# Reading the moving columns of the feed-forward matmuls alternately from the two halves of the operand

## The chip, the cores and the metric

The kernel runs on one core of one Trainium2 chip. The metric is the device time of one execution in microseconds (us), the median of several runs. Beside it stands one execution taken by the hardware profiler, which gives the time of every instruction on each engine: TensorE (PE, with its weight loads as PEld), VectorE (DVE), ScalarE (ACT), GpSimd (POOL) and SyncE (SP), which issues the DMAs.

## The reference

Two stages follow each other. The first is an attention through 32 inducing points over x (4 batches, 12416 rows, 128 channels). The second is a gated feed-forward on its 49664 rows, with 1536 hidden units:

```python
scale = 1.0 / np.sqrt(C)
def mab(q, kv):
    s = scale * (q @ kv.transpose(0, 2, 1))
    s = s - s.max(-1, keepdims=True)
    a = np.exp(s)
    a /= a.sum(-1, keepdims=True) + 1e-09
    return a @ kv
h = mab(I, x)            # 32 inducing rows look at all rows of x
x = mab(x, h).reshape(B * S, D)
g = x @ w_gate
silu = g * (1.0 / (1.0 + np.exp(-g)))
val = x @ w_val
return (silu * val) @ w_out
```

Every row (token) goes through the feed-forward by itself: the order of the tokens does not matter to the arithmetic, so long as the output is put back in order.

## The kernel before

**Layout.** In the feed-forward a token is a column. The attention output is not formed: the 32 weights of a token over the inducing points are put, split in a high and a low part for the 4 row groups, into a tile `stack` of 128 partitions, and the 32 inducing rows are multiplied into the gate and value weights beforehand (tile `tw`, called `st.w`). A matmul of `stack` (the moving operand, streamed column by column) against a 128x128 block of `tw` (the stationary operand, loaded ahead by PEld) gives 128 hidden units of 512 or 480 tokens.

**Tiling.** Each batch has 25 column blocks: 13 of 512 tokens (the first one has 4 x 128) and then 12 of 480. Each block is multiplied in `NT` = 12 steps of 128 hidden units. One such step is a slot:

- `front` (L680) issues two matmuls, the gate (L691) and the value (L692); both read `stack`.
- `gate` has ACT take the SiLU of the gate out of PSUM (L697); `value` has DVE multiply it by the value (L705), which gives `h`.
- `split` rounds `h` to the short format fp32r in `h_hi` (L713, mostly ACT) and subtracts to get the rest, `h_lo` (L715, mostly POOL, one slot in four DVE).
- `back` (L719) issues three matmuls that accumulate in one PSUM tile `o`: `wo_lo` by `h_hi` (L729), `wo_hi` by `h_hi` (L730) and `wo_hi` by `h_lo` (L731). After 12 steps `evac` has DVE copy `o` to `ob` (L738), and SP writes it out.

All five of these matmuls have fp32r operands. The very first block of batch 0 (`u.whole`) is different: its output product is one plain fp32 matmul for each step (L727), which stands in the trace as two MATMUL records.

The moving operands lie without gaps: column k of `stack`, `h_hi` or `h_lo` is the word after column k-1 in each partition. Their tiles are 64 columns wider than needed (`WB`), and start 0 to 48 columns into them, by the table `AT`.

**Order.** The order of the instructions on each engine is written out in the program: slot by slot `front`, `gate`, `value` and the `split` of the slot before, then pieces of the next batch's attention from a list with due slots, then `back` for a slot some 5 to 10 slots older. The first block has its order in the text `SECOND`. Nothing in this order depends on how an operand is addressed. The rest of PE's work is attention: transposes of x (L262), scores (L270), sums over rows (L318, L371) and the projection of the weights (L398, L420).

**Output.** Each block is written as 128 rows of n tokens, and the host's Python turns the blocks into (tokens, 128).

Of the kernel before, what the change touches and what calls it, by code (L numbers as in the profile page):

```python
# [17 lines left out]
B, N, C, M, DFF = 4, 12416, 128, 32, 1536  # L18
P = 128
NG = 4  # L20
NTB = N // NG // 32


def starts(sizes):
# [10 lines left out]
WF = 32 * max(FC)  # L35
WB = WF + 64
AT = (16, 48, 48), (0, 32, 16)
NT = DFF // P
# [14 lines left out]
WP = 512  # L53
# [52 lines left out]
def induced_set_attention_then_swiglu(ctx: ExitStack, tc: tile.TileContext, xt, xn, ind, wgv, wo, out):  # L106
    nc = tc.nc
# [44 lines left out]
    def wcol(k, t):  # L152
        at = WP * (t // 2) + 2 * P * k + P * (t % 2)
        return slice(at, at + P)

    wgv_sb = const.tile([P, 2 * DFF], F32, name="wgv_sb")
    wo_hi = const.tile([P, DFF], F32R, name="wo_hi")
    wo_lo = const.tile([P, DFF], F32R, name="wo_lo")
# [39 lines left out]
    def at(u):  # L198

        return AT[u > NG * FC.count(max(FC))]  # L200
# [10 lines left out]
    def attention(b, one, xn0=None, xt0=None):  # L211
# [5 lines left out]
        def psum(second=0):  # L217
            if xn0 is not None or second:
                return ps_gv.tile([P, 512], F32, name="gv")
            return ps_o.tile([P, 512], F32, name="o")  # L220
# [53 lines left out]
        def s1(q, second=0):  # L274
            if q == 0:
                st.s = one.tile([P, NTB * 32], F32, name="s_all")
                st.mx = att.tile([P, NCH], F32, name="mx")
# [84 lines left out]
        def hacc2(q):  # L362
            g = q >= GA
            n0, n1 = (0, CH0[GA])[g], (CH0[GA], NTB)[g]
            if q in (0, GA):
# [65 lines left out]
        def sl2(b0, b1):  # L431
            return st.s2[:, b0:b1, :]

        def s2_m(b0, b1, second=0):
            if not hasattr(st, "s2"):
                st.s2 = one.tile([P, NTB, M], F32, name="s_all")
            st.sp[b0] = psum(second)
# [16 lines left out]

        def exp2(b0=0, b1=NTB):
            nc.scalar.activation(out=sl2(b0, b1), in_=sl2(b0, b1), func=AF.Exp)
# [166 lines left out]
    start = tc.manual_schedule()  # L623
    start.__enter__()
    s_all = oneb.tile([P, NTB * 32], F32, name="s_all")
    with tc.tile_pool(name="xt0", bufs=NCH - NXT) as xt0, tc.tile_pool(name="xn0", bufs=NCH - NXN) as xn0:
        cur = attention(0, one, xn0, xt0)
        f = cur.f
# [3 lines left out]
        pieces = {}  # L632
# [11 lines left out]
        def run(token):  # L644
            name, *args = token.split(":")
            args = [int(x) if x.isdigit() else x for x in args]
            if name == "ld":
                load_piece(*args)
            elif args and args[0] in pieces:
                getattr(pieces[args[0]], name)(*args[1:])  # L650
            else:
                short[name](*args)
# [27 lines left out]
    def front(st, b, c, t):  # L680
        u = Tile()
        q, j = COLS[c]
        u.b, u.q, u.j, u.t = b, q, j, t
        u.at = at(c)
        n = u.n = WF if q == 0 else 32 * FC[q]

        u.whole = b == 0 and c == 0
        rhs = st.stack[c][:, :n]
        u.g = ps_gv.tile([P, 512], F32, name="gv")
        u.v = ps_gv.tile([P, 512], F32, name="gv")  # L690
        nc.tensor.matmul(out=u.g[:, :n], lhsT=st.w[:, wcol(0, t)], rhs=rhs, start=True, stop=True)  # L691
        nc.tensor.matmul(out=u.v[:, :n], lhsT=st.w[:, wcol(1, t)], rhs=rhs, start=True, stop=True)  # L692
        return u
# [25 lines left out]
    def back(u):  # L719
        n, t = u.n, u.t  # L720
        if t == 0:
            acc["o"] = ps_o.tile([P, 512], F32, name="o")
        o = acc["o"]
        ws = slice(P * t, P * t + P)
        if u.whole:
            k = t % (WP // P)
            nc.tensor.matmul(out=o[:, :n], lhsT=pieces[f"o{t // (WP // P)}"].w[:, P * k:P * k + P], rhs=u.h[:, :n], start=(t == 0), stop=(t == NT - 1))  # L727
        else:
            nc.tensor.matmul(out=o[:, :n], lhsT=wo_lo[:, ws], rhs=u.hi[:, :n], start=(t == 0), stop=False)  # L729
            nc.tensor.matmul(out=o[:, :n], lhsT=wo_hi[:, ws], rhs=u.hi[:, :n], start=False, stop=False)  # L730
            nc.tensor.matmul(out=o[:, :n], lhsT=wo_hi[:, ws], rhs=u.lo[:, :n], start=False, stop=(t == NT - 1))  # L731
        if t == NT - 1:
            evac(u, o)

    def evac(u, o):
        n = u.n
        ob = obp.tile([P, WF], F32, name="ob")
        nc.vector.tensor_copy(out=ob[:, :n], in_=o[:, :n])  # L738
        at = NG * 32 * FC0[u.q] + u.j * n
        nc.sync.dma_start(out=out[u.b, P * at:P * (at + n)].rearrange("(d t) -> d t", d=P), in_=ob[:, :n])  # L740
# [6 lines left out]
    def first(t):  # L747
        made.append(front(cur, 0, 0, t))
        pend.append(made[t])

    short |= dict(f=first, g=lambda t: gate(made[t]), m=lambda t: value(made[t]), k=lambda t: back(pend.pop(0)))
    for token in SECOND.split():
        run(token)
    cur.steps = [(slot, lambda token=token: run(token)) for slot, tokens in FIRST.items() for token in tokens.split()]
    ahead = len(pend)
    for b in range(B):
        nxt = attention(b + 1, (one, oneb)[(b + 1) % 2]) if b + 1 < B else None
        if nxt is not None:
            nxt.steps = plan(nxt, PA if b == 0 else PB)
            if b == 0:  # L760
                cur.steps.append((nxt.e1, lambda: run(f"e2:52:{NTB}")))
                for q in range(2, NF):
# [6 lines left out]
        for slot in range(NT if b == 0 else 0, SLOTS):  # L769
            c, t = slot // NT, slot % NT  # L770
            u = front(cur, b, c, t)
            gate(u)
            value(u)
            u.cast_dve = t in CAST
            u.last = b == B - 1 and slot == SLOTS - 1
            if wait:
                split(wait[0])
                pend.append(wait.pop(0))
            wait.append(u)
            if slot in bursts:  # L780
                u.cast_dve = True
                split(u)
                pend.append(wait.pop(0))
            for a in (cur, nxt):
                while a is not None and a.steps and a.steps[0][0] <= slot:

                    if pend and pend[0].t in getattr(a.steps[0][1], "acc", ()):
                        break
                    a.steps.pop(0)[1]()
            ahead = min(ahead + 1 / RAMP, HI) if nxt is not None and slot < last_burst else max(ahead - 1 / RAMP, SKEW)  # L790
            if slot in bursts:
                ahead = SKEW - (b == 0)
            while len(pend) + len(wait) > ahead:
                back(pend.pop(0))
# [5 lines left out]
    for u in pend + wait:  # L800
        back(u)
# [37 lines left out]
```

## Time and profile before

| | |
|---|---|
| median of 3 runs | 1459.46 us (1459.44 to 1459.61) |
| profiled execution | 1459.38 us |
| its span, first to last instruction | 1457.6 us |
| granted TensorE clock | 1.000 |
| PE busy | 1446.8 us, 99% of the span |
| ACT, POOL, DVE busy | 1278.5, 1208.5, 1195.6 us |
| PEld busy | 1174.3 us |
| matmuls L691, L692 | 1200 each |
| matmuls L729, L730, L731 | 1188 each |
| records of L727 | 24 |

A row of a group gives line, engine and operation, written tile and read tiles, shape, count, busy time and mean time of one. A matmul's time in the profile covers its stream and the way through the array, and it overlaps with the next matmul: the busy time of PE can thus not be read as the sum of single durations. What one matmul costs PE in a dense stretch is the distance from its start to the next one's start, and that is the length of the stretch divided by the count of matmuls in it. In rows of the timeline, instructions of one kind that follow each other stand in one row, with their count.

### The profile page before, as it was taken

How to read it: one execution, taken by the hardware profiler on the slowest of the kernel's cores; microseconds unless marked ns; L12 is line 12 of the kernel's file. 1: busy time of each engine (PE TensorE's matmuls, PEld its weight loads, DVE VectorE, ACT ScalarE, POOL GpSimd, SP SyncE). 2: the span in 40 equal slices, each digit the busy share in tenths (PEclk: the TensorE clock that was granted, in tenths of full speed). 3: DMA queues.
4: the chain of work that ended last, by engine and by line, in shares of the span. 5: the costliest groups of instructions: out<-in, count | busy, mean ns of one | idle time of the engine just before them, and what ended most of it. 6: DMA issues, size and time to landing. Idle time of an engine off the chain costs nothing.

```text
span 1457.6 us, 24926 instructions
## 1 busy us (share of the span) xinstructions
PE 1446.8 (99%) x7452; PEld 1174.3 (81%) x7452; DVE 1195.6 (82%) x2080; ACT 1278.5 (88%) x2388; POOL 1208.5 (83%) x995
## 2 busy tenths in 40 slices
PE   8999999999999999999999999999999999999999
PEld 5577788788887787888888788688888888888887
DVE  6888778887888789888788778987878878878877
ACT  5888898799998887998989888799899999999997
POOL 1689778888998778888899868878889889988987
PEclk9999999999999999999999999999999999999999
DMA  9234522221144242211123522221111111111110
GB/s 370 66 99 127 182 74 99 103 66 54 45 134 138 79 136 105 75 46 41 35 68 114 185 86 87 105 79 42 35 36 41 44 37 37 44 35 40 37 41 21
DMA packets 50822, 119.80 MB, mean 82 GB/s; under 512 B 11392, under 2 KB 28288, under 8 KB 50688
## 3 DMA queue, kind: packets, MB, share of 16 engines
q1 hardware_dynamic: 50688, 118.22, 24.8%
q8 instruction: 59, 0.97, 0.3%
q14 instruction: 75, 0.61, 0.1%
HBM read 62.87 MB, written 25.43 MB: 61 GB/s over the span
## 4 chain that ended last, share of the span: by engine, by line
PE 94%; ACT 2%; DMA 2%; POOL 1%; issue 1%; DVE 0%; SPq 0%; ACTq 0%; DVEq 0%
PE gv L691 18%; PE o L729 18%; PE gv L692 18%; PE o L731 18%; PE o L730 18%; PE gv L270 2%; PE o L318 1%; DMA s_all<-wgv 1%; DMA xt<-xt 1%; PE o L270 1%; PE o L727 1%; ACT silu L697 1%; POOL h_lo L715 1%; ACT h_hi L713 0%; PE gv L420 0%
## 5 line engine op out<-in xcount | busy, mean ns | idle before, releaser
L715 POOL TENSOR_TENSOR h_lo<-h,h_hi 128x512 fp32r<-128x512 f32 (+1 forms) x890 | 1113.2, 1276 | 202.4 <-ACT h_hi L713 142.4
L697 ACT ACTIVATE silu<-gv 128x512 f32<-128x512 f32 (+1 forms) x1200 | 704.2, 588 | 112.5 <-PE gv L691 73.5
L705 DVE TENSOR_TENSOR h<-gv,silu 128x512 f32<-128x512 f32 (+1 forms) x891 | 594.2, 668 | 194.5 <-ACT silu L697 143.8
L713 ACT CAST h_hi<-h 128x512 fp32r<-128x512 f32 (+1 forms) x788 | 475.2, 603 | 29.8 <-DVE h L705 24.6
L691 PE MATMUL gv<-stack,tw 128*128 128x512 f32 (+1 forms) x1200 | 469.0, 391 | 2.0 <-DVE stack L543 1.3
L692 PE MATMUL gv<-stack,tw 128*128 128x512 f32 (+1 forms) x1200 | 463.2, 386 | 0.6 <-ACT silu L697 0.4
L729 PE MATMUL o<-h_hi,wo_lo 128*128 128x512 f32 (+1 forms) x1188 | 460.8, 388 | 0.0
L731 PE MATMUL o<-h_lo,wo_hi 128*128 128x512 f32 (+1 forms) x1188 | 457.6, 385 | 0.0
L730 PE MATMUL o<-h_hi,wo_hi 128*128 128x512 f32 (+1 forms) x1188 | 455.3, 383 | 0.0
L729 PEld LDWEIGHTS o<-h_hi,wo_lo 128*128 128x128 f32 x1188 | 222.6, 187 | 53.9 <-issue 12.1
L691 PEld LDWEIGHTS gv<-stack,tw 128*128 128x128 f32 x1200 | 225.3, 188 | 48.5 <-ACT tw L412 2.6
L692 PEld LDWEIGHTS gv<-stack,tw 128*128 128x128 f32 x1200 | 225.8, 188 | 47.1 <-ACT silu L697 4.0
L731 PEld LDWEIGHTS o<-h_lo,wo_hi 128*128 128x128 f32 x1188 | 223.1, 188 | 42.6 <-POOL h_lo L715 0.4
L730 PEld LDWEIGHTS o<-h_hi,wo_hi 128*128 128x128 f32 x1188 | 223.1, 188 | 41.1
L705 DVE TENSOR_TENSOR gv<-gv,silu 128x512 f32<-128x512 f32 (+1 forms) x297 | 201.7, 679 | 40.5 <-ACT silu L697 39.3
L715 DVE TENSOR_TENSOR h_lo<-gv,h_hi 128x512 fp32r<-128x512 f32 (+1 forms) x297 | 197.5, 665 | 1.8 <-ACT h_hi L713 0.2
L713 ACT CAST h_hi<-gv 128x512 fp32r<-128x512 f32 (+1 forms) x294 | 167.4, 570 | 10.0 <-DVE gv L705 8.8
L738 DVE COPY ob<-o 128x512 f32<-128x512 f32 (+1 forms) x100 | 66.4, 664 | 0.8 <-PE o L731 0.8
L713 DVE CAST h_hi<-h 128x512 fp32r<-128x512 f32 (+1 forms) x103 | 60.6, 589 | 0.0
L483 POOL TENSOR_TENSOR a_lo<-aT,a_hi 128x480 fp32r<-128x480 f32 (+2 forms) x26 | 32.6, 1253 | 0.0
L190 POOL TENSOR_TENSOR wgv_sb<-s_all 128x512 int32<-128x512 int32 x2 | 2.9, 1456 | 28.8 <-ACT s_all L178 28.8
L467 POOL TENSOR_TENSOR s_all<-s_all,sm 128x512 f32<-128x512 f32 (+2 forms) x27 | 26.1, 967 | 0.0
(155 smaller groups left out, 476.5 us busy)
## 6 DMA issues: line engine op xcount, KB each, us to landing
xt_sb<-xt SPq DMA_DIRECT2D x32, 896.0 KB, 5.3
xn_sb<-xn SPq DMA_DIRECT2D x18, 896.0 KB, 5.9
out<-ob SPq DMA_DIRECT2D x52, 256.0 KB, 2.0
out<-ob SPq DMA_DIRECT2D x48, 240.0 KB, 2.0
stack<-a_hi SPq DMA_DIRECT2D x96, 64.0 KB, 2.0
stack<-a_lo SPq DMA_DIRECT2D x96, 64.0 KB, 2.0
stack<-a_hi SPq DMA_DIRECT2D x96, 60.0 KB, 2.0
stack<-a_lo SPq DMA_DIRECT2D x96, 60.0 KB, 2.0
```

The source lines that it names most:

```text
L270: nc.tensor.matmul(out=ps[32 * j:32 * j + 32, 32 * (lo - b0):32 * (hi - b0)], lhsT=lhsT, rhs=st.xt[q][:, lo - CH0[q]:hi - CH0[q], j, :], s ...
L483: eng.tensor_sub(out=st.al[q][:, :n], in0=st.at[q][:, :n], in1=st.ah[q][:, :n].bitcast(F32))
L691: nc.tensor.matmul(out=u.g[:, :n], lhsT=st.w[:, wcol(0, t)], rhs=rhs, start=True, stop=True)
L692: nc.tensor.matmul(out=u.v[:, :n], lhsT=st.w[:, wcol(1, t)], rhs=rhs, start=True, stop=True)
L697: nc.scalar.activation(out=u.s[:, :u.n], in_=u.g[:, :u.n], func=AF.Silu)
L705: nc.vector.tensor_mul(out=u.h[:, :n], in0=u.v[:, :n], in1=u.s[:, :n])
L713: (nc.vector.tensor_copy if u.cast_dve else nc.scalar.copy)(out=u.hi[:, :n], in_=u.h[:, :n])
L715: eng.tensor_sub(out=u.lo[:, :n], in0=u.h[:, :n], in1=u.hi[:, :n].bitcast(F32))
L729: nc.tensor.matmul(out=o[:, :n], lhsT=wo_lo[:, ws], rhs=u.hi[:, :n], start=(t == 0), stop=False)
L730: nc.tensor.matmul(out=o[:, :n], lhsT=wo_hi[:, ws], rhs=u.hi[:, :n], start=False, stop=False)
L731: nc.tensor.matmul(out=o[:, :n], lhsT=wo_hi[:, ws], rhs=u.lo[:, :n], start=False, stop=(t == NT - 1))
L738: nc.vector.tensor_copy(out=ob[:, :n], in_=o[:, :n])
```

## The change

A helper `turns` gives the same n columns of an operand in another order: column 0 of the first half, column 0 of the second half, column 1 of the first half, and so on. The moving operand of all five feed-forward matmuls, and of the plain fp32 one of the first block, goes through it. Two reads that follow each other are thus n/2 columns apart: 1024 bytes for 512 columns, 960 bytes for 480. PSUM is written as before, without gaps, so the result of `front` has its tokens in the turned order, and `back` turns them once more. The tiles, their places, the stationary operands, and what ACT, DVE, POOL and SP do stay. The host undoes both turns when it reads the output.

```diff
+def turns(x):
+
+    return x.rearrange("p (a b) -> p b a", a=2)
...
-        rhs = st.stack[c][:, :n]
+        rhs = turns(st.stack[c][:, :n])
         u.g = ps_gv.tile([P, 512], F32, name="gv")
         u.v = ps_gv.tile([P, 512], F32, name="gv")
         nc.tensor.matmul(out=u.g[:, :n], lhsT=st.w[:, wcol(0, t)], rhs=rhs, start=True, stop=True)
...
-            nc.tensor.matmul(out=o[:, :n], lhsT=pieces[f"o{t // (WP // P)}"].w[:, P * k:P * k + P], rhs=u.h[:, :n], start=(t == 0), stop=(t == NT - 1))
+            nc.tensor.matmul(out=o[:, :n], lhsT=pieces[f"o{t // (WP // P)}"].w[:, P * k:P * k + P], rhs=turns(u.h[:, :n]), start=(t == 0), stop=(t == NT - 1))
         else:
-            nc.tensor.matmul(out=o[:, :n], lhsT=wo_lo[:, ws], rhs=u.hi[:, :n], start=(t == 0), stop=False)
-            nc.tensor.matmul(out=o[:, :n], lhsT=wo_hi[:, ws], rhs=u.hi[:, :n], start=False, stop=False)
-            nc.tensor.matmul(out=o[:, :n], lhsT=wo_hi[:, ws], rhs=u.lo[:, :n], start=False, stop=(t == NT - 1))
+            hi, lo = turns(u.hi[:, :n]), turns(u.lo[:, :n])
+            nc.tensor.matmul(out=o[:, :n], lhsT=wo_lo[:, ws], rhs=hi, start=(t == 0), stop=False)
+            nc.tensor.matmul(out=o[:, :n], lhsT=wo_hi[:, ws], rhs=hi, start=False, stop=False)
+            nc.tensor.matmul(out=o[:, :n], lhsT=wo_hi[:, ws], rhs=lo, start=False, stop=(t == NT - 1))
...
-        blk = o[:, P * NG * 32 * c0:P * NG * 32 * (c0 + c)]
+        n = WF if c0 == 0 else 32 * c
+        turn = np.arange(n).reshape(2, n // 2).T.reshape(-1)
+        back = np.argsort(turn[turn])
+        blk = o[:, P * NG * 32 * c0:P * NG * 32 * (c0 + c)].reshape(B, -1, P, n)[..., back]
```

The order of the instructions of every engine, and what each waits for, is row by row the same before and after, apart from the line numbers: the gate and the value stand at L696 and L697 after (before L691 and L692), the three output products at L735 to L737 (before L729 to L731), the plain fp32 one at L732 (before L727), and the lines of ACT, DVE and POOL between them are 5 higher. Only the addresses in these six lines differ.

## The prediction, as it was put on record

> **What bounds the kernel now.** I read the page's engine shares first, then the chain of waits, then the waits of PE, to see which engine sets the end.
>
> ```profile
> PE 1446.8 (99%) x7452; PEld 1174.3 (81%) x7452; DVE 1195.6 (82%) x2080; ACT 1278.5 (88%) x2388; POOL 1208.5 (83%) x995
> ...
> PE 94%; ACT 2%; DMA 2%; POOL 1%; issue 1%; DVE 0%; SPq 0%; ACTq 0%; DVEq 0%
> PE gv L691 18%; PE o L729 18%; PE gv L692 18%; PE o L731 18%; PE o L730 18%; PE gv L270 2%; PE o L318 1%; DMA s_all<-wgv 1%; DMA xt<-xt 1%; PE o L270 1%; PE o L727 1%; ACT silu L697 1%; POOL h_lo L715 1%; ACT h_hi L713 0%; PE gv L420 0%
> ```
>
> The second and third rows say that the chain that ended last runs over PE for 94% of the span, and that 90% of it are the five feed-forward products, which the change rewrites. PE hardly waits for anyone: of 1457.6 us it is idle for 10.8. So whatever one of these products costs more or less appears in full, as many times as it is issued, until another engine becomes the bound.
>
> The groups by shape give the counts. Their mean times overlap and can't be summed.
>
> ```profile
> L691 PE MATMUL gv<-stack,tw 128*128 128x512 f32 x624 | 248.3, 398 | 2.0 <-DVE stack L543 1.3 <-ACT tw L412 0.2 <-DVE h L705 0.2
> L692 PE MATMUL gv<-stack,tw 128*128 128x512 f32 x624 | 244.2, 391 | 0.6 <-ACT silu L697 0.4 <-DVE h L705 0.2
> L729 PE MATMUL o<-h_hi,wo_lo 128*128 128x512 f32 x612 | 240.9, 394 | 0.0
> L730 PE MATMUL o<-h_hi,wo_hi 128*128 128x512 f32 x612 | 238.6, 390 | 0.0
> L731 PE MATMUL o<-h_lo,wo_hi 128*128 128x512 f32 x612 | 238.5, 390 | 0.0
> L691 PE MATMUL gv<-stack,tw 128*128 128x480 f32 x576 | 220.7, 383 | 0.0
> L729 PE MATMUL o<-h_hi,wo_lo 128*128 128x480 f32 x576 | 219.9, 382 | 0.0
> L731 PE MATMUL o<-h_lo,wo_hi 128*128 128x480 f32 x576 | 219.1, 380 | 0.0
> L692 PE MATMUL gv<-stack,tw 128*128 128x480 f32 x576 | 219.0, 380 | 0.0
> L730 PE MATMUL o<-h_hi,wo_hi 128*128 128x480 f32 x576 | 216.7, 376 | 0.0
> ```
>
> That is 624 + 624 + 3 x 612 = 3084 products of 512 columns and 5 x 576 = 2880 of 480.
>
> What one costs is the length of a dense stretch over its count. In the last batch there is no attention beside it; its first stretch below holds only products of 512 columns, the second only of 480.
>
> ```profile
> 1130.00:1290.00 160.00, 160.00 (x707) 132.53 (x706) 131.10 (x216) 147.97 (x271) 142.49 (x112) 1.00 0.13 40
> 1310.00:1450.00 140.00, 140.00 (x642) 120.29 (x641) 113.54 (x192) 127.36 (x246) 121.59 (x101) 1.00 0.11 34
> ```
>
> The columns are the stretch, its length, then busy time and count of PE, PEld, DVE, ACT and POOL, the granted clock, the DMA share and GB/s. A product of 512 columns costs 160.00 / 707 = 226.3 ns, one of 480 costs 140.00 / 642 = 218.1 ns, at the full granted clock. ACT is the next engine, 92% busy in the first stretch and 91% in the second; it leaves PE the bound, but not by much.
>
> **The slower stream that this trace holds.** The plain fp32 product of the first block and the transposes also read 128 partitions without gaps, and stream at another rate.
>
> ```profile
> L727 PE MATMUL o<-h_hi,s_all x16: 590/592/592, 50.7 to 60.6; 128*128 128x512 f32 x16
> ...
> L262 PE MATMUL gv<-ident,xt_sb x56: 272/273/331, 5.4 to 17.8; 128*128 128x128 f32 x56
> ...
> 50.74 1.02 PE L727 MATMUL o<-h_hi,s_all 128*128 128x512 f32 x2
> ```
>
> The first two rows have the shortest, the median and the longest of the single times. 384 more columns take 592 - 273 = 319 ns, which is 0.831 ns a column. In the timeline's row two records of L727 cover 1.02 us; with 0.592 for the second alone, they start 428 ns apart, which is 512 x 0.831 = 425.5 and 2.5 ns more. The fp32r products stream almost twice as fast: 226.3 / 512 = 0.442 ns a column. If they ran at exactly twice that slower rate, 512 columns would cost 512 x 0.4155 + 2.5 = 215.2 ns and 480 would cost 201.9. They take 11.1 and 16.2 ns more. So the fast stream doesn't quite keep up with itself even where its words lie side by side. I take this as the sign that reading the moving operand, not the array, is near its limit there.
>
> **The change part by part.** It adds and removes no instruction, no DMA and no wait, and every queue has the same rows in the same order; the helper and the host's index cost the device nothing, since nothing on any engine or queue stands for them. What is left is one price: a moving column that doesn't lie beside the one read before it.
>
> No matmul of this trace reads that way. (L270 reads runs of 32 columns, but only at the slower rate.) So I bound the price. Below, it is nothing: the fetch might hold on to both places, and might even gain from them, as a rival below says. Above, the nearest rows are two reductions on DVE over the same 128 columns of `ident`, one along the row (L133), one with a step of 32 words (L129).
>
> ```profile
> L129 DVE TENSOR_REDUCE fold<-ident 128x32 f32<-128x128 f32 x1 | 0.4, 374 | 1.8 <-POOL ident masks.py:199 1.8
> L133 DVE TENSOR_REDUCE group<-ident 128x4 f32<-128x128 f32 x1 | 0.3, 278 | 0.0
> ...
> L206 DVE TENSOR_REDUCE sm<-pairs 128x16 f32<-128x32 f32 x12 | 2.2, 186 | 0.4
> L206 DVE TENSOR_REDUCE sm<-pairs 128x4 f32<-128x8 f32 x3 | 0.5, 162 | 0.1
> ```
>
> The two L206 rows show that an element costs (186 - 162) / 24 = 1.0 ns whether there are more results or fewer, so the 28 more results of L129 don't explain its 96 ns. The step does: 96 / 128 = 0.75 ns more for each word, 1.79 ns in place of about 1.04. Words that don't lie together are dearer to fetch on that engine, by a factor of 1.7.
>
> [...]
>
> For the forecast I take the price at which PE gets one column in the time of two: the 0.831 ns that a column costs in L727. I choose it since it is the one slower rate at which PE is seen to stream, and since 0.442 times DVE's factor of 1.7 is 0.76, close to it.
>
> - 512 columns: 428 - 226.3 = 201.7 ns more, x 3084 = 622 us.
> - 480 columns: 480 x 0.831 + 2.5 = 401.4; less 218.1 is 183.3 ns more, x 2880 = 528 us.
> - The 24 records of L727 already stream at that rate: nothing. (At DVE's 1.79 ns a column they would cost 24 x 0.49 = 12 us.)
>
> No cover has to hold for this: ACT, DVE, POOL and PEld have 1279 us or less to do and would stand idle half of the time. The sum is 1459.4 of the profiled execution (span 1457.6 and 1.8 around it, 0.1 below the median) and 1150, which makes 2609 us.
>
> **Rivals.**
>
> *A column pays as on DVE.* With 0.75 ns added to each column, 512 x 0.75 = 384 ns x 3084 and 360 ns x 2880 give 2221 us more: 3681. With the whole 1.79 ns for each column, (916 - 226) x 3084 and (859 - 218) x 2880 give 3974 more: 5433. For it speaks that the contiguous stream takes 4 x 0.442 = 1.77 ns for four words, just DVE's time for one that lies alone; against it, that PE fetches four words in the time in which DVE fetches fewer than two.
>
> *One width pays.* The two places are 1024 bytes apart for 512 columns and 960 for 480. If memory is split by address, one distance may meet itself and the other not. Only 512 at the half rate: 1459 + 622 = 2081; only 480: 1987. A change of some ns at the seams would be in this case too: with 5 ns on each of 5964 it is 1489. For it speaks that 480 columns are 16.2 ns over the doubled slow rate and 512 only 11.1, so that something other than the number of columns counts.
>
> [...]
>
> *Faster: the other side.* The 11.1 and 16.2 ns are time in which one place in memory is asked too often; two places in turn would let one rest while the other answers. It decides from the point where both lines are held and PE is given its next column at 0.4155 ns: 11.1 x 3084 + 16.2 x 2880 = 81 us less, 1378. ACT would then be busy for 147.97 / 160 / 0.951 = 97% of the first stretch and 98% of the second, and its waits would show; I put this case at half of the gain, 1419. For it speaks that the excess stands in every fp32r stretch and in none of the slow ones; against it the DVE rows.
>
> **How the numbers follow.** The half rate has 0.31, the dearer column 0.17, one width or small prices 0.12, nothing 0.11, faster 0.29. The forecast is the likeliest, 2609 us; its own range is 2458 to 2754, from 0.78 to 0.88 ns a column. Slower by over 0.2% (about what a measurement of this kernel can tell from no change) is 0.31 + 0.17 + 0.12 = 0.60, within 0.2% 0.11, faster 0.29. For 8 times in 10 the range has to go from most of the faster case over the small ones to the half rate: 1400 to 2760. It leaves out the dearer column and the last part of the faster case.
>
> **What would show it.** If the forecast holds, the dense stretches have about 428 and 401 ns for each product, single times of the products near 590 ns, as L727 has, L727 itself unchanged, ACT near half busy, and PE still without idle time. A dearer column shows as 600 to 920 ns for each product. One width shows as two stretches that part. In the faster case the stretches fall toward 215 and 202 ns, with ACT as what PE begins to wait for. The forecast is wrong from its root if single times of 512 columns stay near 390 ns: then a column far from the last one costs PE's fetch nothing.

## The result: 4.3% faster, where 79% slower was forecast

The changed kernel takes 1397.11 us (median of 4 runs, 1397.04 to 1398.15), the kernel before 1459.53 us. The ratio is 0.957, with a 95% interval from 0.9555 to 0.9588. The forecast was 2609 us, and the time lies just below the range that was given. The profiled execution took 1398.15 us with a span of 1396.4, which is 61.2 us less than the one before. Now and then a single execution of either kernel takes a multiple of the time (2923.87 us once for a changed kernel, 8262.44 and 2923.93 us for the kernel before), and such executions are left out of the ranges.

The page of the changed kernel, its engine shares and the chain that ended last:

```profile
PE 1381.0 (99%) x7452; PEld 1177.1 (84%) x7452; DVE 1184.5 (85%) x2080; ACT 1254.6 (90%) x2388; POOL 1193.8 (85%) x995
...
PE 92%; ACT 3%; DVE 2%; DMA 1%; issue 1%; POOL 0%; SPq 0%; DVEq 0%; ACTq 0%
PE gv L697 17%; PE o L737 17%; PE o L735 17%; PE gv L696 17%; PE o L736 17%; PE gv L275 2%; ACT h_hi L718 1%; ACT silu L702 1%; DMA xt<-xt 1%; PE o L323 1%; PE o L732 1%; DVE h L710 1%; PE o L275 1%; POOL h_lo L720 0%; PE gv L425 0%
```

PE is still the bound, over the same five products, and it has 66 us less to do. The counts of instructions are the same. Two groups by shape, and the two dense stretches of the last batch (length, then busy time and count of PE, PEld, DVE, ACT and POOL, clock, DMA share, GB/s; in the first stretch ten of the 718 products still have 480 columns, which moves the mean by 0.2 ns):

```profile
L696 PE MATMUL gv<-stack,tw 128*128 128x512 f32 x624 | 242.9, 389 | 2.4 <-DVE stack L548 0.8 <-ACT silu L702 0.6 <-DVE h L710 0.6
...
L696 PE MATMUL gv<-stack,tw 128*128 128x480 f32 x576 | 210.9, 366 | 0.0
...
1075.00:1230.00 155.00, 155.00 (x718) 134.91 (x717) 132.47 (x219) 146.66 (x276) 143.37 (x114) 1.00 0.14 41
1255.00:1390.00 135.00, 135.00 (x665) 124.77 (x664) 114.94 (x199) 128.24 (x255) 122.48 (x104) 1.00 0.12 37
```

A product of 512 columns now costs 155.00 / 718 = 215.9 ns (226.3 before), one of 480 costs 135.00 / 665 = 203.0 ns (218.1 before). A column that lies a kilobyte from the one read before it costs nothing more; on the contrary, the products lose nearly all of the time that they had over twice the slow rate (215.2 and 201.9 by the prediction's sum).

One product went the other way. The two records of a step of the plain fp32 product of the first block, single times and a pair in the timeline:

```profile
L732 PE MATMUL o<-h_hi,s_all x16: 700/703/705, 52.4 to 63.7; 128*128 128x512 f32 x16
...
52.38 1.24 PE L732 MATMUL o<-h_hi,s_all 128*128 128x512 f32 x2
```

They start 1240 - 703 = 537 ns apart, against 428 before.

**Where the gain went.** By the dense stretches, 3084 x 10.4 ns and 2880 x 15.1 ns are 32.1 + 43.5 = 75.6 us. The span became only 61.2 us shorter: 14.4 us are missing. The first of them were lost ahead of the feed-forward. Its first product starts 1.4 us later in this execution, in which a transfer of x came late. Before and after:

```profile
37.34 0.50 PE L691 MATMUL gv<-stack,tw 128*128 128x512 f32 x1 [1.26 <-DVE stack L543]
```

```profile
21.07 0.91 PE L275 MATMUL gv<-xt,indT 128*32 128x416 f32 x8 [1.18 <-DMA xt<-xt]
...
38.73 0.48 PE L696 MATMUL gv<-stack,tw 128*128 128x512 f32 x1 [0.82 <-DVE stack L548]
```

That is not the change: when the same kernel was run again (last experiment below), its first product started at 37.55 us. The 24 records of the plain fp32 product are 24 x 109 ns = 2.6 us late, and about 1.5 us of this reaches the products behind them: from the first L691 to the L692 at 67.43 us it is 30.09 us before, and from the first L696 to the same product (L697 at 70.31) it is 31.58. About 11.5 us are left. PE's idle time went from 10.8 to 1396.4 - 1381.0 = 15.4 us. And weight loads wait longer for the other engines. Waits in the kernel before (besides, 1.2 us of L692 for DVE and 0.4 of L731 for POOL):

```profile
PEld gv L692 <- ACT silu L697: 4.0, 13, 0.8
```

and in the changed kernel (us in all, times, the longest):

```profile
PEld gv L697 <- ACT silu L702: 9.6, 27, 0.8
PEld o L737 <- POOL h_lo L720: 8.8, 30, 0.5
PEld gv L697 <- DVE h L710: 4.0, 9, 0.9
```

PE has come close to ACT, DVE and POOL, and where attention work lies in between, they are now late at times. It fits that the last batch, which has none, loses nearly nothing: from a product at its start (1130.49 us before, 1087.41 after) to the end, 18.2 of the 18.5 us that its counts give were gained. The rows explain the size roughly; how much of a weight load's wait reaches the end was not split further.

### The profile page after: what moved, and what is told of

Same layout as the page of the kernel before. It is cut to its first block, busy times and chain, and to the rows that moved or that the text cites. A ratio compares the mean times of both kernels' runs of the same rounds, so it can differ in the third digit from the quotient of the medians.

```text
span 1396.4 us, 24926 instructions
## 1 busy us (share of the span) xinstructions
PE 1381.0 (99%) x7452; PEld 1177.1 (84%) x7452; DVE 1184.5 (85%) x2080; ACT 1254.6 (90%) x2388; POOL 1193.8 (85%) x995
## 4 chain that ended last, share of the span: by engine, by line
PE 92%; ACT 3%; DVE 2%; DMA 1%; issue 1%; POOL 0%; SPq 0%; DVEq 0%; ACTq 0%
PE gv L697 17%; PE o L737 17%; PE o L735 17%; PE gv L696 17%; PE o L736 17%; PE gv L275 2%; ACT h_hi L718 1%; ACT silu L702 1%; DMA xt<-xt 1%; PE o L323 1%; PE o L732 1%; DVE h L710 1%; PE o L275 1%; POOL h_lo L720 0%; PE gv L425 0%
## 5 line engine op out<-in xcount | busy, mean ns | idle before, releaser
L720 POOL TENSOR_TENSOR h_lo<-h,h_hi 128x512 fp32r<-128x512 f32 (+1 forms) x890 | 1098.1, 1258 | 153.8 <-ACT h_hi L718 100.1
L696 PE MATMUL gv<-stack,tw 128*128 128x512 f32 (+1 forms) x1200 | 453.8, 378 | 2.4 <-DVE stack L548 0.8
L697 PE MATMUL gv<-stack,tw 128*128 128x512 f32 (+1 forms) x1200 | 450.7, 376 | 3.6 <-ACT silu L702 1.8
L737 PE MATMUL o<-h_lo,wo_hi 128*128 128x512 f32 (+1 forms) x1188 | 446.0, 375 | 0.1
L735 PE MATMUL o<-h_hi,wo_lo 128*128 128x512 f32 (+1 forms) x1188 | 445.4, 375 | 0.0
L736 PE MATMUL o<-h_hi,wo_hi 128*128 128x512 f32 (+1 forms) x1188 | 442.8, 373 | 0.0
L697 PEld LDWEIGHTS gv<-stack,tw 128*128 128x128 f32 x1200 | 226.6, 189 | 41.6 <-ACT silu L702 9.6
L696 PEld LDWEIGHTS gv<-stack,tw 128*128 128x128 f32 x1200 | 226.7, 189 | 35.0 <-issue 3.1
L735 PEld LDWEIGHTS o<-h_hi,wo_lo 128*128 128x128 f32 x1188 | 224.5, 189 | 35.1 <-issue 12.1
L737 PEld LDWEIGHTS o<-h_lo,wo_hi 128*128 128x128 f32 x1188 | 224.4, 189 | 33.6 <-POOL h_lo L720 8.8
L736 PEld LDWEIGHTS o<-h_hi,wo_hi 128*128 128x128 f32 x1188 | 224.5, 189 | 23.4
L718 DVE CAST h_hi<-h 128x512 fp32r<-128x512 f32 (+1 forms) x103 | 52.6, 511 | 0.0
```

Of the source, the lines that this page charges most:

```text
L718: (nc.vector.tensor_copy if u.cast_dve else nc.scalar.copy)(out=u.hi[:, :n], in_=u.h[:, :n])
L720: eng.tensor_sub(out=u.lo[:, :n], in0=u.h[:, :n], in1=u.hi[:, :n].bitcast(F32))
L735: nc.tensor.matmul(out=o[:, :n], lhsT=wo_lo[:, ws], rhs=hi, start=(t == 0), stop=False)
L736: nc.tensor.matmul(out=o[:, :n], lhsT=wo_hi[:, ws], rhs=hi, start=False, stop=False)
L737: nc.tensor.matmul(out=o[:, :n], lhsT=wo_hi[:, ws], rhs=lo, start=False, stop=(t == NT - 1))
```

## Experiments

Three theories stood at the start for why reading in turns is faster; they were the author's suppositions, which the traces of the two kernels did not show. *Place*: two places in memory far apart let one rest while the other answers (the prediction's faster rival). *Line*: four neighbouring columns of a partition, 16 bytes, called a line here, are fetched together, and it is enough that two lines are in use, so that one is fetched while the other serves. *Step*: reading the very next word is what is slow. Against all of them stood the forecast's price for a lone column. Where no range or count is given, a kernel was executed once.

### Only the gate and the value in turns

```diff
-            ... rhs=turns(u.h[:, :n]) ...          # L732
+            ... rhs=u.h[:, :n] ...
-            hi, lo = turns(u.hi[:, :n]), turns(u.lo[:, :n])
+            hi, lo = u.hi[:, :n], u.lo[:, :n]
```

> Only the gate and the value product read in turns; the three output products and the plain fp32 one read word after word. If the gain lies in the stream of each product by itself, the gate and the value cost 215.9 ns (512 columns) and 203.0 (480) as in the changed kernel, the output products 226.3 and 213 to 220 as before, and two fifths of the 62 us are gained: about 1434 us. If the gain lies at the seam between two products (the last word of one, the first of the next), the seams that stay plain stay dear and those between a turned and a plain product change by themselves: single distances then don't split by the product that streams.

It took 1436.97 us (one run; before 1459.66 on that chip). Starts of PE's products, from the timeline (start, time, instruction):

```profile
1149.95 0.38 PE L696 MATMUL gv<-stack,tw 128*128 128x512 f32 x1
1150.17 0.38 PE L697 MATMUL gv<-stack,tw 128*128 128x512 f32 x1
1150.38 0.39 PE L735 MATMUL o<-h_hi,wo_lo 128*128 128x512 f32 x1
1150.62 0.39 PE L736 MATMUL o<-h_hi,wo_hi 128*128 128x512 f32 x1
1150.85 0.40 PE L737 MATMUL o<-h_lo,wo_hi 128*128 128x512 f32 x1
1151.08 0.38 PE L696 MATMUL gv<-stack,tw 128*128 128x512 f32 x1
```

From L696 and L697 the next start is 0.22 and 0.21 us away, from L735, L736 and L737 it is 0.24, 0.23 and 0.23. The two turned products are at the new pace and the three plain ones are not, so the gain is in the stream of each product by itself. The plain ones are a few ns slower than in the kernel before, so the gain is a little under two fifths: 22.7 us.

### The two places 16 and 64 bytes apart

```diff
-    return x.rearrange("p (a b) -> p b a", a=2)
+    return x.rearrange("p (c a b) -> p c b a", a=2, b=4)     # 16 bytes; b=16 for 64 bytes
```

> All products read in turns, but from two places only 16 bytes apart: columns 0 4 1 5 2 6 3 7, then the next 8. Theory 'place' (two distant places in memory let one rest while the other answers): the places are too near, no gain, about 1459 us, 226.3 and 218.1 ns. Theory 'line' (16 bytes are fetched at once, and a second open line hides the fetch of the next): full gain at any distance, about 1397 us, 215.9 and 203.0 ns. Theory 'step' (reading the very next word is what is slow): full gain too, 1397 us. If two lines can't be held: over 2600 us.

> As the one before, with the two places 64 bytes apart: columns 0 16 1 17 and so on in pieces of 32. 'Place': full gain (1397 us) if memory is split in pieces of 64 bytes or less, none (1459 us) if in larger ones. 'Line' and 'step': full gain, 1397 us. Between the two: a split that helps at some seams only, 1410 to 1445 us.

1396.27 and 1396.32 us. The stretch of 512 columns and that of 480 with 16 bytes:

```profile
1100.00:1235.00 135.00, 135.00 (x624) 117.34 (x623) 116.33 (x193) 127.60 (x240) 125.44 (x100) 1.00 0.13 40
1250.00:1380.00 130.00, 130.00 (x640) 120.10 (x639) 110.45 (x192) 123.28 (x245) 118.27 (x100) 1.00 0.12 37
```

That is 216.3 and 203.1 ns, the full gain, out of two places 16 bytes apart; with 64 bytes it is 135.00 / 625 = 216.0 and 130.00 / 640 = 203.1 ns. *Place* falls as it was meant: the halves need not be far apart.

### Every fourth column

```diff
-    return x.rearrange("p (a b) -> p b a", a=2)
+    return x.rearrange("p (b a) -> p a b", a=4)
```

> Every fourth column, four times over: columns 0 4 8 ... then 1 5 9 ... Each read comes from another 16 bytes than the one before, in rising order, and comes back to a line only a quarter of the product later. 'Line': no line is used twice while open, so each column pays a fetch: at 1.77 ns a column (226.3 / 128) 906 ns for 512 columns and over 5000 us; at the half rate that was forecast 428 ns and about 2600 us. 'Step': 215.9 ns, 1397 us. 'Place': the stream passes every place four times as fast, so between 1397 and 1459 us.

2805.73 us. Its stretches, and the plain fp32 product:

```profile
2180.00:2470.00 290.00, 290.00 (x630) 131.28 (x629) 123.57 (x194) 132.87 (x242) 128.47 (x101) 1.00 0.06 19
...
57.84 1.98 PE L732 MATMUL o<-h_hi,s_all 128*128 128x512 f32 x2
L732 PE MATMUL o<-h_hi,s_all x16: 1078/1081/1083, 57.8 to 78.1; 128*128 128x512 f32 x16
```

A product of 512 columns costs 460.3 ns, 0.90 ns a column. So the forecast's price exists, at 0.90 in place of the 0.83 that was taken for it, when each column lies 16 bytes past the one read before it. *Step* falls. The plain fp32 product is hit too: its records start 1980 - 1081 = 899 ns apart, against 428.

### Even columns first; another order within a line; whole lines in turn

```diff
-    return x.rearrange("p (a b) -> p b a", a=2)
+    return x.rearrange("p (b a) -> p a b", a=2)              # 0 2 4 6 ... 1 3 5 7 ...
+    return x.rearrange("p (c a b) -> p c b a", a=2, b=2)     # 0 2 1 3, 4 6 5 7 ...
+    return x.rearrange("p (a b w) -> p b a w", a=2, w=4)     # 0 1 2 3 256 257 258 259 ...
```

(one of the three lines in each run)

> Even columns first, then odd ones: 0 2 4 6 ... 1 3 5 7 ... The next read is never the very next word, each line of 16 bytes gives two words in a row, and only one line is in use at a time. 'Step' (the very next word is what is slow): full gain, about 1396 us. 'Line' (two lines in use, each used several times, hide the fetches): no gain. With 460.5 ns for 512 fetches in the run of every fourth column, one fetch is 0.90 ns, so 256 fetches of two words are 230 ns: about as before or a little slower, 1455 to 1490 us.

> Columns 0 2 1 3, 4 6 5 7 and so on: the order changes only within a line of 16 bytes, and one line follows the other as before. 'Step': gain, at least where the step isn't one word (three of four reads), 1396 to 1415 us. 'Line': one line in use at a time and four uses of it in a row, as before: 1459 us, 226 and 218 ns.

> Whole lines in turn: columns 0 1 2 3 of the first half, then 0 1 2 3 of the second, then 4 5 6 7 of the first. 'Line' in its strict form (two lines have to be in use at once, word by word): no gain, 1459 us. If it is enough that the next line lies elsewhere in memory, so that lines that follow each other aren't neighbours: full gain, 1396 us. That would bring back 'place' for neighbouring lines only.

2741.26, 1461.51 and 1553.46 us. The stretch of 512 columns in each, in this order:

```profile
2130.00:2420.00 290.00, 290.00 (x644) 133.54 (x643) 125.31 (x196) 135.94 (x248) 132.50 (x103) 1.00 0.06 19
```

```profile
1145.00:1290.00 145.00, 145.00 (x641) 120.09 (x641) 119.58 (x198) 133.95 (x246) 130.32 (x103) 1.00 0.13 40
```

```profile
1215.00:1375.00 160.00, 160.00 (x641) 120.96 (x640) 124.45 (x198) 138.57 (x246) 130.00 (x102) 1.00 0.12 37
```

450.3, 226.2 and 249.6 ns. Another order within four neighbouring columns makes no difference (226.2 ns against 226.3), although only one read in four is of the very next word: that speaks against *step* once more. Whole lines in turn are slower than before (249.6), so it is not the neighbourhood of lines that costs. The even columns were missed by far: 230 ns were expected of a price for each line fetched, and 256 lines that give two words in a row are as dear as 512 that give one each (450.3 and 460.3 ns). Both theories missed the whole lines in turn (1459 or 1396 us).

### A shorter weight load

The excess of 10.4 and 15.1 ns could also come from the weight load that runs beside each stream (187 to 188 ns each in the kernel before). In the kernel before, the middle one of the three output products got 32 stationary columns in place of 128:

```diff
-            nc.tensor.matmul(out=o[:, :n], lhsT=wo_lo[:, ws], rhs=u.hi[:, :n], start=(t == 0), stop=False)
-            nc.tensor.matmul(out=o[:, :n], lhsT=wo_hi[:, ws], rhs=u.hi[:, :n], start=False, stop=False)
+            nc.tensor.matmul(out=o[:, :n], lhsT=wo_hi[:, ws], rhs=u.hi[:, :n], start=(t == 0), stop=False)
+            nc.tensor.matmul(out=o[:32, :n], lhsT=wo_lo[:, P * t:P * t + 32], rhs=u.hi[:, :n], start=False, stop=False)
```

> The kernel before, with words read one after another; only the product of the low output weights is now the second of the three, and has 32 stationary columns in place of 128 (it leaves out three quarters of the rows of that correction). Its weight load, which runs while the product before it (the first of the three, L729) streams, reads a quarter of the words. Theory 'load' (the moving stream loses about 10 ns to the weight load beside it, whatever its length): L729 to L730 falls from 226 and 219 ns to about 218 and 206, the four other distances stay. Theory 'stream alone' (the stream of single lines is slow by itself): all distances stay within 2 ns.

1467.21 us. The load was shorter, the stream beside it not:

```profile
L730 PEld LDWEIGHTS o<-h_hi,wo_lo 128*32 128x32 f32 x1188 | 128.2, 108 | 43.2
...
1200.73 0.39 PE L729 MATMUL o<-h_hi,wo_hi 128*128 128x512 f32 x1
1200.95 0.40 PE L730 MATMUL o<-h_hi,wo_lo 128*32 128x512 f32 x1
1201.19 0.39 PE L731 MATMUL o<-h_lo,wo_hi 128*128 128x512 f32 x1
```

The load of the low output weights fell from 187 to 108 ns. L729 to L730 is 0.22 to 0.23 us in these rows; over all of them the middle one of the starts in the trace is 226 ns at 512 columns and 213 at 480, where 218 and 206 were expected (227 and 220 in the kernel before, read in the same way). Other distances rose by up to 9 ns, which neither theory foresaw. For 512 columns the weight load is not what costs; for 480, where half of the expected fall is there, its part stays open.

### Two columns of each half in turn; four quarters in turn

By now the author's theory was that PE asks for two columns at a time and that any new line among them costs one answer of 1.77 ns, the time of four columns word after word, 4 x 0.442 ('answer').

```diff
-    return x.rearrange("p (a b) -> p b a", a=2)
+    return x.rearrange("p (a b w) -> p b a w", a=2, w=2)     # 0 1 256 257 2 3 258 259 ...
+    return x.rearrange("p (a b) -> p b a", a=4)              # 0 128 256 384 1 129 ...
```

(one of the two in each run)

> Two columns of the first half, then two of the second: 0 1 256 257 2 3 258 259. Theory 'answer' (formed from the runs so far): PE reads two columns at a time; when either lies in a new line of 16 bytes, memory takes about 1.77 ns to answer, for one new line or two at once; the reads that follow from lines already held run at 0.42 ns a column and hide it. Word after word, each four columns need one answer and take 4 x 0.42 = 1.67 ns, a little too few to hide 1.77. In the changed kernel two lines are asked for together and then serve eight columns, 3.37 ns. Here the two new lines are asked for one after the other, two answers for eight columns again: 8 columns take 3.54 ns, 226 and 218 ns a product, about 1459 us. Theory 'line' (it is enough that two lines are in use): 215.9 and 203.0 ns, 1396 us.

> One column of each of four quarters in turn: 0 128 256 384 1 129 257 385. 'Answer' with four lines held: two answers for 16 columns, full gain, 215.9 and 203.0 ns, 1396 us. 'Answer' with only two lines held: each pair of columns needs an answer, 1.77 ns for two columns, 453 and 425 ns, about 2740 us, as in the run of the even columns.

2030.71 and 1738.46 us: both theories miss both. The stretch of 512 columns of the one, and of the other with its plain fp32 product:

```profile
1585.00:1795.00 210.00, 210.00 (x641) 125.35 (x640) 125.36 (x196) 135.23 (x247) 130.18 (x103) 1.00 0.09 27
```

```profile
1360.00:1540.00 180.00, 180.00 (x636) 121.30 (x636) 125.81 (x197) 134.72 (x244) 129.89 (x102) 1.00 0.11 32
...
54.15 1.90 PE L732 MATMUL o<-h_hi,s_all 128*128 128x512 f32 x2
L732 PE MATMUL o<-h_hi,s_all x16: 1032/1040/1048, 54.2 to 71.3; 128*128 128x512 f32 x16
```

327.6 and 283.0 ns. Here the plain fp32 product helped, which reads the same pattern in each run, word after word at about half the pace (428 ns for 512 columns, against 226.3). Split each order of columns into those at even places and those at odd places. In the change, the even places hold 0 1 2 3 ... of the first half and the odd ones the same of the second: each has four words in a row from a line. Word after word, the even places hold 0 2 | 4 6 | ...: two in a row. Of the even columns they hold 0, 4, 8, ...: one. In pairs of columns, and in quarters, the places of one kind meet two lines in alternation. From this the author made the theory 'two readers': each kind of place is fetched by itself, and it costs what the plain fp32 product, as a single reader, pays for such a sequence. It is a way to count the measured times; no trace shows a reader.

### The same halves in turn, with two words in a row for each reader

```diff
-    return x.rearrange("p (a b) -> p b a", a=2)
+    return x.rearrange("p (a b e) -> p e b a", a=2, e=2)     # 0 256 2 258 4 260 ... 1 257 3 259 ...
```

> The two halves in turn as in the change, but even columns first and then the odd ones: 0 256 2 258 4 260 ... then 1 257 3 259. The same two places, one column of each in turn, but a line of 16 bytes now gives two words in a run in place of four. Theory 'two readers': one reader fetches the columns at even places of the order, a second one those at odd places, each as the plain fp32 product fetches all of its columns: 0.84 ns a word with four words in a row from a line, 0.88 to 0.92 with two, 1.75 to 1.80 with one, 1.05 where two lines alternate. Here each reader gets two words in a row: 0.88 to 0.92 ns a word, 226 to 235 ns for 512 columns and 213 to 222 for 480, about 1455 to 1490 us, though both halves are still read in turn. The plain fp32 product has one reader, which meets two lines in alternation with two uses each, as each of the two readers does in the run of two columns and two columns: 1.30 ns a word, its records about 666 ns apart. Theory 'line' (enough that two lines are in use): full gain, 1396 us.

1452.84 us. Its stretches and its plain fp32 product:

```profile
1140.00:1285.00 145.00, 145.00 (x641) 120.08 (x640) 119.57 (x198) 133.98 (x245) 130.32 (x103) 1.00 0.13 40
1300.00:1440.00 140.00, 140.00 (x658) 122.99 (x657) 114.24 (x196) 130.42 (x253) 123.51 (x103) 1.00 0.12 36
...
53.51 1.47 PE L732 MATMUL o<-h_hi,s_all 128*128 128x512 f32 x2
L732 PE MATMUL o<-h_hi,s_all x16: 811/819/822, 53.5 to 66.8; 128*128 128x512 f32 x16
```

226.2 ns at 512 columns, just what the kernel before has word after word, and 212.8 at 480. The halves are still read in turn, and the gain at 512 columns is gone. The fp32 records start 1470 - 819 = 651 ns apart (666 expected). *Line* falls, and so does any form of *place*, since two distant places still take turns. 'Two readers' gave both numbers beforehand, within 3%; the whole time is 2 us below its range.

The prices of one word for one reader, counted by this theory, from the distance of the products over half of their columns (512 wide), and of the plain fp32 records over all of theirs:

| words that a reader gets from a line | fp32r product, ns a word | plain fp32, ns a word |
|---|---|---|
| four in a row | 0.843 (the change) | 0.836 (before, 428 / 512) |
| two in a row | 0.884 (before; and the last run) | 0.92 (even columns, 470 / 512) |
| two in a row, then a distant line | 0.975 (whole lines in turn) | 0.91 (two and two, 466 / 512) |
| one | 1.76 (even columns), 1.80 (every fourth) | 1.756 (every fourth) |
| two lines alternating, four each | 1.105 (quarters) | 1.049 (the change) |
| two lines alternating, two each | 1.28 (two and two) | 1.27 (the last run) |

The 470 and 466 ns are from the run of the even columns and that of two and two. The second record of a pair has the shortest single time there, so that 1080 - 610 and 1080 - 614 are the distances of the starts:

```profile
53.40 1.08 PE L732 MATMUL o<-h_hi,s_all 128*128 128x512 f32 x2
L732 PE MATMUL o<-h_hi,s_all x16: 610/620/632, 53.4 to 66.7; 128*128 128x512 f32 x16
```

```profile
51.68 1.08 PE L732 MATMUL o<-h_hi,s_all 128*128 128x512 f32 x2
L732 PE MATMUL o<-h_hi,s_all x16: 614/618/627, 51.7 to 63.3; 128*128 128x512 f32 x16
```

That four words, 16 bytes, count as one line rests on these rows: the plain fp32 record pays 0.92 ns a word where each lies 8 bytes past the one before (even columns) and 1.756 where it lies 16 bytes past (every fourth), and a reader of the fp32r product about the same at 16 bytes (1.76, even columns) and 32 (1.80, every fourth).

The two columns were measured on different instructions and agree within 6% over a factor of two, but for the third row. Only the two figures of the last run were foretold by the theory; it was formed from the others. What stays open: whole lines in turn, where each reader gets two in a row and then a distant line, cost 0.975 ns a word, 7% more than the plain fp32 record pays for that sequence, so the theory misses something there; why the 480 columns took 218.1 ns in the kernel before and 212.8 in the last run; and what the readers are in the machine, which no trace shows.

### The plain fp32 product left as it was; one more rounding on DVE

The price list says that the plain fp32 product should not be turned. With that undone (the host's index accounts for it), and in a second kernel with one more of the twelve roundings of a block given to DVE in place of ACT:

```diff
-            ... rhs=turns(u.h[:, :n]) ...          # L732
+            ... rhs=u.h[:, :n] ...
-CAST = {11}
+CAST = {3, 11}                                     # the second kernel only
```

> The changed kernel, but the plain fp32 product of the first block reads word after word as before. Its 24 records, 537 ns apart within a pair in the changed kernel and 428 before, fall back to 428: 24 x 109 ns = 2.6 us less where PE is the bound, 1394.5 us. Rival: in that first stage ACT and DVE are late anyway and take the time back, 1397 us, no difference.

> As the one before, and DVE takes two of the twelve roundings of a block (step 3 beside step 11) from ACT. If the rest of the gain went into waits for ACT (busy for 95% of the dense stretches of the changed kernel, where DVE has 85%), PE waits less: 1388 to 1392 us. Rival: DVE, which also reads the value out of PSUM, becomes what is late, and the time stays or rises: 1395 to 1402 us.

The first took 1395.41 us (1395.21 to 1395.63), a ratio of 0.955 (0.9537 to 0.9571) to the kernel before, between its two expectations. The second took 1415.56 us, 0.969 (0.9676 to 0.9707): it is 20 us slower than the first, more than its rival allowed (1402 us), since PE now waits longer for ACT and POOL. Waits of its weight loads and of ACT:

```profile
ACT h_hi L718 <- DVE gv L710: 55.5, 86, 1.4
...
PEld gv L697 <- ACT silu L702: 25.8, 73, 0.8
PEld o L737 <- POOL h_lo L720: 17.4, 41, 0.8
```

ACT's roundings wait for DVE's products (55.5 us, against 5.0 in the changed kernel), and what ACT does next comes late to PE (25.8 us, against 9.6). The rest of the gain can't be had by giving this rounding to DVE.

The changed kernel and the first of the two were then run on one chip:

> The changed kernel itself, to stand beside the next one on the same chip: 1397 us, within 1 us.

> The changed kernel with the plain fp32 product of the first block read word after word. Its own run gave 1395.4 us, on another chip than the changed kernel's. If the 24 records are worth what they were late, it is 1.5 to 2.6 us below the changed kernel here; if that was the chip, the two are the same within 0.5 us.

The changed kernel took 1396.78 to 1397.20 us (4 runs), the other 1395.23 to 1396.14 (3 runs). The runs don't overlap, and the medians differ by 1.8 us. The starts say the same: from the first feed-forward product to the one that is at 67.43 us in the kernel before it is 31.6 us in the changed kernel and 30.1 in the other. So some 1.5 of the 2.6 us reach the end. That is 0.1% of the time, and clear only for this chip and these few runs.

## Why the prediction was wrong

**The bound: right.** PE sets the end, and what one of the 5964 products costs appears for the greater part: 75.6 us by the stretches, 61.2 in the span. That no instruction is added or moved was right as well; waits that were there before became longer.

**The price of a column: this step failed.** The prediction took a column that isn't beside the one read before it to cost "the time of two", 0.831 ns, and so 1150 us. That price is real, and stands in the run of the even columns and in that of every fourth (0.88 and 0.90 ns a column, 2741 and 2806 us). But the change doesn't pay it: a column costs 215.9 / 512 = 0.422 ns in it, less than the 0.442 before, and the single times stay at 389 ns, which the prediction had named as the sign of being wrong from its root. What the prediction counted was that no column lies beside the one read before it. By the theory that the runs leave, the read in between goes to the other reader, and what counts is how many words in a row a reader gets from a line: there the change went from two to four (0.884 to 0.843 ns a word), not down to one (1.76).

**The row from DVE: rightly read, wrongly carried over.** A lone word costs DVE 1.79 ns by the prediction's estimate from two single rows, and by the count with two readers PE 1.76 to 1.80. The prediction noted that PE's four words take 1.77 ns, and counted it only as a point for the dearer rival. Counted with two readers, it is the price of one line for each of them, of which they use two words: by that theory, a part of the price stood already in the kernel before. No trace shows the wait itself.

**The sign that was seen.** The prediction found 11.1 and 16.2 ns over twice the slow rate in each fp32r product and took reading, not the array, to be near its limit. That held: 10.4 and 15.1 ns were gained by another order of reading alone. The faster rival built on it had nearly the right amount (81 us), but not the cause (two distant places; 16 bytes are enough, 1396.27 us). No run shows the two lines that are "held" in its sum; what the runs showed is 215.9 and 203.0 ns a product, where the sum has 215.2 and 201.9. It supposed that ACT would take half of the gain, where some 11.5 us of 75.6, about a seventh, went into the stages in which it and its neighbours have attention work too. With 0.29 it was close behind the forecast's 0.31.

**The plain fp32 product: wrong.** "Nothing" was taken for its 24 records; they cost 109 ns more each (537 against 428) with the halves in alternation, 2.6 us in all; about 1.5 us of it reached the end.

## What to carry to other kernels

Where fp32r products bound a kernel and their distances lie some per cent over half of what a plain fp32 product of the shape takes (here 226.3 ns against 428 / 2 = 214), try an order of the moving operand in which the columns at even places are neighbours and those at odd places are neighbours, for example two halves in turn; here it took the products to 215.9 ns and cost no instruction, only an index where the result leaves. Do it for fp32r products alone: the plain fp32 products of the same shape became 25% slower with it here (537 ns against 428). And before the price of one stream is carried over to another order of columns, look at which of the measured streams already pays a part of it.

## What the runs showed of the hardware that was not expected

- A stream of fp32r columns word after word is not the fastest one: 226.3 ns for 512 columns, against 215.9 to 216.3 with two places in turn, each read word after word, be they 16 bytes (216.3), 64 bytes (216.0) or a kilobyte (215.9) apart. With two places in turn, each read at every second word, it is 226.2.
- The measured times of an fp32r product can be counted as if two readers fetched its columns, those at even and those at odd places, and each paid what a plain fp32 record pays for the same sequence of words, within 6% in five sequences and 7% in a sixth. No trace shows the readers.
- A lone word from a line costs about the same, 1.76 to 1.80 ns, for a plain fp32 record (899 / 512), for half of the columns of an fp32r product (450.3 / 256 and 460.3 / 256) and, by the prediction's estimate from two single rows, in DVE's reduction (1.79).
- With four places in alternation a plain fp32 record takes 1900 - 1040 = 860 ns for 512 columns, 1.68 ns a word, nearly the price of a lone word (1.756); two places in alternation cost 1.05. Why the step lies between two and four was not shown.
